# Expert routing of a fused DeltaNet + MoE kernel: started one period later, and its weights computed on GpSimd instead of VectorE

## The chip, the cores and the metric

One NeuronCore of a Trainium2 chip runs the whole kernel. Its engines work side by side, each through its own queue of instructions in program order: TensorE (PE in the profile; PEld is its weight load), VectorE (DVE), ScalarE (ACT), GpSimd (POOL) and SyncE (SP, which issues DMA transfers). The metric is the device time of one execution in microseconds (us).

## The reference

Two blocks follow each other. The first is DeltaNet attention, a recurrence over 768 time steps for 4 batches of 8 heads with head size 48:

```python
for t in range(S):
    kt, vt, bt = (k_n[:, :, t], v[:, :, t], beta[:, :, t, None])
    y[:, :, t] = np.einsum('bhd,bhde->bhe', q[:, :, t], state)
    v_old = np.einsum('bhde,bhd->bhe', state, kt)
    state = state + bt[:, :, :, None] * np.einsum('bhd,bhe->bhde', kt, vt - v_old)
```

Its output, reordered to 3072 tokens of width 384, goes through a two-level mixture of experts. A token picks the best of 4 groups (largest of 4 logits) and, inside the group, the best of 4 experts; its weight is the product of the two softmax values at those places:

```python
g_idx = np.argmax(g_logits, axis=1)      # g_sm = softmax(g_logits), with + 1e-09 in the divisor
e_idx = np.argmax(e_logits, axis=1)      # e_sm = softmax(e_logits), the same
h = np.maximum(xg[mask_e] @ w1[g, e], 0.0)
ye = h @ w2[g, e]
combined = g_w[mask_g][mask_e] * e_w[mask_e]
out[tok_idx] = combined[:, None] * ye
```

## The kernel before

**Stages.** Attention is computed in chunks of 32 time steps, 24 chunks, called u = 0 to 23. One chunk holds 4 batches x 32 steps = 128 tokens. After it the MoE stage goes through the 16 experts one after the other. Between them lies a DRAM array, `x_dram`, that holds the tokens sorted by expert: a token's row is written there by an indirect DMA, and the MoE stage reads an expert's rows from it. The MoE stage can't start before the last of these writes has landed.

**A period of attention.** The loop at L512 emits one *period* per chunk, and one more for the last routing work. Inside a period the work is emitted in a fixed order: the matmuls of chunk u (`advance`, L264: `a_ps`, `o_ps`, then `w_ps`, then `s_ps` and the state `s_bd`, then `o_ps` and the output `x`), the router logits of chunk u - 1 (`logits`, L328: transposes `t_ps`, copy `xt`, matmuls `l_ps`, copy `lg`), the value scaling `vh` of chunk u + 1 (`scale`, L257, on VectorE), and the Gram matrices of chunk u + 9 (`gram`, L162: matmuls `g_ps`, ScalarE copy `gt`, VectorE product `gq`, L184). The tensors `t_ps`, `g_ps` and `r_ps` share one PSUM buffer with the tag "g", so each must be read out before the next is written.

**The elimination.** Every four chunks form a group g, and for each group VectorE inverts the triangular 32x32 systems of the four chunks (`inverse`, L188): a transpose of `gt` into `m` (L194), a clamp (L199), a square root on ScalarE (L201), some short steps, then thirty pairs `t` = product (L233) and `m` += `t` (L237), each waiting for the one before it, a last product (L239) and a transpose into `mt` (L244). ScalarE turns that into `mtb` (L249), which `w_ps` of the group's chunks reads.

**Routing.** The chunks are routed in groups r: r = 0 to 4 of four chunks, r = 5 and 6 of two. `route` (L347) reads the group's logits `lg`, takes maxima `gb`, `eb`, makes one-hot masks `gh`, `eh` (ties broken by the descending constant `desc`), the differences `sx` = (`gx`, `ex`), the joint mask `hot`, and adds `hot` to the running counts `acc` (GpSimd for groups of four, L398). TensorE counts ranks into `r_ps` (L404, L405), ScalarE takes `sx` = exp(`sx`) (L407), VectorE makes the slots `rk`, `slot_i` (L410, L413) and the weight `cw` (L417 to L429: sums `ed`, `gd`, products, a reciprocal). GpSimd copies `cw` into the token rows (L436) and issues the indirect DMA that scatters them (L437); these writes are called *puts* here. GpSimd also writes the row numbers into `x` (L318). There are ten `x` buffers, so a chunk's put must have landed before the chunk ten later writes its `x`.

**What sets the order.** All engines' orders inside attention are written out by hand. `inverse` and `route` are Python generators, kept in a list `behind`; each `yield` is a place where the task may be left. `work(n)` (L464) gives every task n x 180 x share nanoseconds of credit, and pushes tasks by one step while they have credit; a step costs 180, or more where the yield says so. A task that yields a word (`ACT_STEP`, `PE_STEP`, `SOON`, `NEXT`) is held until the loop calls `allow` with it: `NEXT` right after the first part of `advance` in the next period, `PE_STEP` and `ACT_STEP` near a period's end. So an emitted place fixes the order in each engine's queue, and what stands ahead in a queue blocks what is behind it. A routing task starts at the end of the period after its group's last chunk, with share 0.25, or 0.6 and 1 for the last groups:

```python
r = group_of.get(u - 1)
if r is not None and group_of.get(u) != r:
    start(route(r), 0.25 if r < NGR - 2 else 0.6 if r < NGR - 1 else 1)
```

NGR is 6. Where the text names "period 5" it means the pass of the loop with u = 5.

Of the kernel before, what the change touches and what calls it, by code (L numbers as in the profile page):

```python
# [8 lines left out]
F32 = mybir.dt.float32  # L9
I32 = mybir.dt.int32  # L10
AX = mybir.AxisListType
ALU = mybir.AluOpType
# [42 lines left out]
def deltanet_then_moe(  # L55
# [14 lines left out]
    nc = tc.nc  # L70
# [15 lines left out]
    NGR = NCH // RG  # L86
# [33 lines left out]
    with ExitStack() as first:  # L120
        ap_ = first.enter_context(tc.tile_pool(name="attn", bufs=1))
        wk = first.enter_context(tc.tile_pool(name="wk", bufs=2))
        sm = first.enter_context(tc.tile_pool(name="small", bufs=2))
# [201 lines left out]
        group_of = {u: r for r, (u0, n) in enumerate(groups) for u in range(u0, u0 + n)}  # L325
# [21 lines left out]
        def route(r):  # L347


            u0, n = groups[r]  # L350
            us = range(u0, u0 + n)

            def small(name, shape_, dt=F32):
                return sm.tile([128, RG] + shape_, dt, tag=name, name=f"{name}{r}",
                               bufs=3)[:, 0:n]

            lg = lg_.pop(r)[:, 0:n]
            gl, el = lg[:, :, 0:G], lg[:, :, G:NL].rearrange("p n (g e) -> p n g e", g=G)
            gb, eb = small("gb", [1]), small("eb", [G])
            gh, eh = small("gh", [G]), small("eh", [G, EG])  # L360
            gt, et = small("gt", [1]), small("et", [G])
            sx = small("sx", [NL])
            gx, ex = sx[:, :, 0:G], sx[:, :, G:NL].rearrange("p n (g e) -> p n g e", g=G)
            like_g, like_e = [128, n, G], [128, n, G, EG]
            desc_g = cut["desc"].rearrange("p (n e) -> p n e", n=RG)[:, 0:n]
            desc_e = cut["desc"][:, None, 0:G * EG].to_broadcast([128, n, G * EG]).rearrange(
                "p n (g e) -> p n g e", g=G)
            nc.vector.tensor_reduce(gb[:, :, 0], gl, axis=AX.X, op=ALU.max)
            yield
            nc.vector.tensor_reduce(eb, el, axis=AX.X, op=ALU.max)  # L370
            yield
            nc.vector.tensor_tensor(gh, gl, gb.to_broadcast(like_g), op=ALU.is_ge)
            yield
            nc.vector.tensor_tensor(eh, el, eb[:, :, :, None].to_broadcast(like_e), op=ALU.is_ge)
# [9 lines left out]
            nc.vector.tensor_tensor(gh, gh, gt.to_broadcast(like_g), op=ALU.is_equal)  # L384
            yield
            nc.vector.tensor_tensor(eh, eh, et[:, :, :, None].to_broadcast(like_e),
                                    op=ALU.is_equal)
            yield
            nc.vector.tensor_tensor(gx, gl, gb.to_broadcast(like_g), op=ALU.subtract)
            yield  # L390
            nc.vector.tensor_tensor(ex, el, eb[:, :, :, None].to_broadcast(like_e),
                                    op=ALU.subtract)
            yield
            hot = small("hot", [G, EG])
            nc.vector.tensor_tensor(hot, gh[:, :, :, None].to_broadcast(like_e), eh, op=ALU.mult)  # L395
            hotf = hot.rearrange("p n g e -> p n (g e)")
            for g, u in enumerate(us):
                (nc.gpsimd if n == RG else nc.vector).tensor_tensor(  # L398
                    acc[:, u + 1], acc[:, u], hotf[:, g], op=ALU.add)
            if n == RG:  # L400
                yield NEXT
            yield PE_STEP
            r_ps = ps.tile([128, RG, NE], F32, tag="g", name=f"r_ps{r}")[:, 0:n]
            nc.tensor.matmul(r_ps, lhsT=before, rhs=hotf, start=True, stop=False)  # L404
            nc.tensor.matmul(r_ps, lhsT=ones, rhs=acc[:, u0:u0 + n], start=False, stop=True)  # L405
            yield ACT_STEP
            nc.scalar.activation(sx, sx, ACT.Exp)  # L407
            yield NEXT
            rk, slot_i = small("rk", [NE]), small("slot_i", [1], I32)
            nc.vector.tensor_tensor(rk, r_ps, hotf, op=ALU.mult)  # L410
            yield
            with nc.allow_low_precision("sums of whole numbers below 2 ** 24"):
                nc.vector.tensor_reduce(slot_i[:, :, 0], rk, axis=AX.X, op=ALU.add)  # L413
            yield

            gd, ed, cw = small("gd", [1]), small("ed", [G]), small("cw", [1])
            nc.vector.tensor_reduce(ed, ex, axis=AX.X, op=ALU.add)  # L417
            yield
            nc.vector.tensor_reduce(gd[:, :, 0], gx, axis=AX.X, op=ALU.add)
            yield  # L420
            nc.vector.scalar_tensor_tensor(ed, in0=ed, scalar=1e-9, in1=gh, op0=ALU.add,
                                           op1=ALU.mult)
            yield
            nc.vector.tensor_reduce(cw[:, :, 0], ed, axis=AX.X, op=ALU.add)
            yield
            nc.vector.scalar_tensor_tensor(cw, in0=gd, scalar=1e-9, in1=cw, op0=ALU.add,
                                           op1=ALU.mult)
            yield
            nc.vector.reciprocal(cw, cw)  # L429
            yield  # L430
            for g, u in enumerate(us):
                x = xs.pop(u)
                if n == RG:
                    yield
                    yield
# [15 lines left out]
        def start(task, share):  # L451
            behind.append(task)
            rate[task], due[task] = share, 0.0
# [32 lines left out]
        with tc.manual_schedule(engines={mybir.EngineType.PE, mybir.EngineType.DVE,  # L486
# [25 lines left out]
            for u in range(NCH + 1):  # L512
                step = advance(u) if u < NCH else iter([None] * 4)
                turned = logits(u - 1) if u else iter([None] * 2)
                next(step)
                allow(NEXT)
                next(turned)
                if u + 1 < NCH:
                    scale(u + 1)
                work(8)  # L520
                if u % RG == RG - 1 and u // RG + 2 < NGR:
                    start(inverse(u // RG + 2), 1)
                work(8)
# [12 lines left out]
                if r is not None and group_of.get(u) != r:  # L536
                    start(route(r), 0.25 if r < NGR - 2 else 0.6 if r < NGR - 1 else 1)
                allow(SOON)
                work(12)
                if u + NB < NCH:  # L540
                    load_kq(u + NB)
                if u + NV < NCH:
                    load_kv(u + NV)
                if u in (2, 3):
                    weights[u - 2] = load_expert(u - 2)
                if u == 1:
                    for e in range(NE):
                        nc.sync.dma_start(out=slots(e), 
                                          in_=zero[:, None, :].to_broadcast([P, T, XW]))
# [118 lines left out]
    with tc.For_i(0, n_over):  # L668
# [10 lines left out]
                                       op0=ALU.mult, op1=ALU.add)  # L679
# [83 lines left out]
```

## Time and profile before

The median of three runs is 642.9 us (639.74 to 643.19). The profile comes from one further execution that took 636.67 us; its span, from the first to the last instruction, is 634.9 us.

| what | where in the span | us |
|---|---|---|
| set-up and first elimination | 0 to 56 | 56 |
| periods 0 to 3 | 56 to 104 | 48 |
| periods 4 to 7 | 104.77 to 147.45 | 42.7 |
| periods 8 to 11 | 147.45 to 187.81 | 40.4 |
| periods 12 to 15 | 187.81 to 227.21 | 39.4 |
| periods 16 to 19 | 227.21 to 261.16 | 34.0 |
| periods 20 to 23 | 261.16 to 291.80 | 30.6 |
| last routing, puts landing | 291.80 to 304.88 | 13.1 |
| experts | 304.88 to 634.9 | 330.0 |

A period's bounds are the starts of the ScalarE copy `f` (L280). Over the span TensorE is busy 520.8 us, VectorE 248.5, ScalarE 177.9 and GpSimd 75.4. In a timeline a line reads: start, duration, engine, line, operation, output <- inputs, shape, and in brackets the idle time of that engine just before and what ended it. "issue" stands for idle time that no recorded event explains.

### The profile page before, as it was taken

How to read it: one execution, taken by the hardware profiler on the slowest of the kernel's cores; microseconds unless marked ns; L12 is line 12 of the kernel's file. 1: busy time of each engine (PE TensorE's matmuls, PEld its weight loads, DVE VectorE, ACT ScalarE, POOL GpSimd, SP SyncE). 2: the span in 40 equal slices, each digit the busy share in tenths (PEclk: the TensorE clock that was granted, in tenths of full speed). 3: DMA queues.
4: the chain of work that ended last, by engine and by line, in shares of the span. 5: the costliest groups of instructions: out<-in, count | busy, mean ns of one | idle time of the engine just before them, and what ended most of it. 6: DMA issues, size and time to landing. Idle time of an engine off the chain costs nothing. (4 is left out here: it accounts for less than half of the span.)

```text
span 634.9 us, 18041 instructions
## 1 busy us (share of the span) xinstructions
PE 520.8 (82%) x8070; PEld 476.2 (75%) x8070; DVE 248.5 (39%) x744; ACT 177.9 (28%) x336; POOL 75.4 (12%) x136
## 2 busy tenths in 40 slices
PE   2313768888889788883799999999999999999991
PEld 2203546766667666673699999999999999999990
DVE  5688976869959699223011111101111111111000
ACT  2102334474555645541011111111111111111110
POOL 4000000020030301305000111001110001110011
PEclk9999989898979879996699999999999999999996
DMA  8960787353331221302245755656656557556000
GB/s 214 266 208 1 211 261 271 96 145 88 96 107 62 67 75 61 111 4 101 65 158 182 237 180 191 212 153 225 226 159 213 171 189 239 176 198 203 26 15 20
DMA packets 39551, 93.40 MB, mean 147 GB/s; under 512 B 3465, under 2 KB 24002, under 8 KB 39472
## 3 DMA queue, kind: packets, MB, share of 16 engines
q1 hardware_dynamic: 35888, 82.76, 41.7%
q0 software_dynamic: 3584, 9.47, 4.2%
q8 instruction: 64, 1.05, 0.7%
q14 instruction: 15, 0.12, 0.1%
HBM read 77.21 MB, written 15.78 MB: 146 GB/s over the span
## 5 line engine op out<-in xcount | busy, mean ns | idle before, releaser
L597 PE MATMUL h_ps<-xt,w 128*128 128x224 f32 x768 | 155.2, 356 | 0.6 <-DVE xt L588 0.6
L611 PE MATMUL y_ps<-hid,w 128*128 128x224 f32 x768 | 153.3, 353 | 0.0
L597 PEld LDWEIGHTS h_ps<-xt,w 128*128 128x128 f32 x768 | 144.7, 193 | 1.4 <-DVE xt L588 0.9
L611 PEld LDWEIGHTS y_ps<-hid,w 128*128 128x128 f32 x768 | 143.0, 190 | 0.0
L588 DVE COPY xt<-t_ps 128x336 f32<-128x336 f32 x32 | 16.2, 508 | 167.5 <-PE t_ps L586 167.5
L600 ACT ACTIVATE hid<-h_ps 128x448 f32<-128x448 f32 x64 | 34.8, 543 | 140.4 <-PE h_ps L597 140.4
L625 DVE TENSOR_SCALAR yo<-o_ps,xg 112x384 f32<-112x384 f32 x32 | 19.7, 618 | 120.4 <-PE o_ps L622 120.4
L626 POOL DMA_INDIRECT out_dram<-yo,at x32 | 30.1, 941 | 296.9 <-DVE yo L625 237.1
L237 DVE TENSOR_TENSOR m<-m,t 128x30 f32<-128x30 f32 (+9 forms) x180 | 59.6, 331 | 5.1
L233 DVE TENSOR_TENSOR t<-m 128x30 f32<-128x30 f32 (+9 forms) x180 | 59.4, 330 | 4.4
L270 PE MATMUL a_ps<-vh,con 128*128 128x384 f32 x48 | 27.9, 670 | 36.8 <-DVE vh L257 23.9
L613 ACT ACTIVATE yt<-y_ps 128x224 f32<-128x224 f32 x48 | 17.1, 357 | 134.3 <-PE y_ps L611 134.3
L176 PE MATMUL g_ps<-kqt 48*32 48x64 f32 x1536 | 25.3, 260 | 23.1 <-issue 9.5
L308 ACT ACTIVATE s_bd<-s_ps 48x768 f32<-48x768 f32 x46 | 36.9, 803 | 19.6 <-PE s_ps L302 19.0
L176 PEld LDWEIGHTS g_ps<-kqt 48*32 48x32 f32 x1536 | 19.8, 124 | 26.6 <-issue 12.3
L270 PEld LDWEIGHTS a_ps<-vh,con 128*128 128x128 f32 x48 | 8.8, 230 | 39.2 <-DVE vh L257 21.2
L302 PE MATMUL s_ps<-w,kv 32*128 32x96 f32 x736 | 27.8, 286 | 7.5 <-ACT w L295 4.7
L302 PEld LDWEIGHTS s_ps<-w,kv 32*128 32x128 f32 x736 | 23.8, 192 | 10.1 <-ACT w L295 5.7
L292 PEld LDWEIGHTS w_ps<-f,mtb 64*64 64x64 f32 x768 | 25.7, 140 | 7.6 <-issue 5.3
L276 PEld LDWEIGHTS a_ps<-s_bd,kqt 128*32 128x32 f32 x736 | 18.7, 128 | 16.5 <-issue 16.5
L292 PE MATMUL w_ps<-f,mtb 64*64 64x48 f32 x768 | 28.8, 226 | 2.4 <-issue 1.2
L398 POOL TENSOR_TENSOR acc<-acc,hot 128x16 f32<-128x16 f32 x20 | 6.1, 306 | 188.5 <-DVE hot L395 187.4
(92 smaller groups left out, 489.5 us busy)
## 6 DMA issues: line engine op xcount, KB each, us to landing
w<-in_w_dram SPq DMA_DIRECT2D x32, 1536.0 KB, 6.8
kv<-in_kv_dram SPq DMA_DIRECT2D x24, 448.0 KB, 3.8
kqt<-in_kq_dram SPq DMA_DIRECT2D x48, 192.0 KB, 6.6
x_dram<-zero SPq DMA_DIRECT2D x16, 337.8 KB, 8.0
xg<-x_dram SPq DMA_DIRECT2D x16, 337.8 KB, 3.2
con<-in_const_dram SPq DMA_DIRECT2D x1, 755.0 KB, 4.8
out_dram<-yo,at POOLq DMA_INDIRECT x32, 3.5
x_dram<-x,slot_i POOLq DMA_INDIRECT x24, 3.2
```

Of the source, the lines that this page charges most:

```text
L176: nc.tensor.matmul(g_out[quads[b], hh * NP + j], lhsT=kqt[rows, 0, j, quads[b]], rhs=kqt[rows, :, j, quads[b]], start=True, stop=True, ski ...
L233: nc.vector.tensor_tensor(tv, m[:, j + 1:, j:j + 1].to_broadcast([128, n, j]), m[:, j:j + 1, 0:j].to_broadcast([128, n, j]), op=ALU.mult)
L237: nc.vector.tensor_tensor(m[:, j + 1:, 0:j], m[:, j + 1:, 0:j], tv, op=ALU.add)
L270: nc.tensor.matmul(a_ps.rearrange("p h d -> p (h d)"), lhsT=ident, rhs=vh.rearrange("p h d -> p (h d)"), start=True, stop=(u == 0), skip_g ...
L292: nc.tensor.matmul(w_ps[b, h], lhsT=mt[b, uu * H + (h % 2) * NP + h // 2], rhs=f[b, h], start=True, stop=True, skip_group_check=True)
L302: nc.tensor.matmul(s_at[:, b, j], lhsT=k[quads[b], j], rhs=w[quads[b], 2 * j:2 * j + 2], start=(u == 0 and j == 0), stop=True, skip_group_ ...
L308: nc.scalar.activation(s_bd[rows, :, :, hh, :], s_at[rows, :, :, hh * D:(hh + 1) * D], ACT.Copy)
L597: nc.tensor.matmul(h_ps[:, k], lhsT=w1[:, j, (f + k) * 128:(f + k + 1) * 128], rhs=xt[:, j], start=(j == 0), stop=(j == DC - 1), skip_grou ...
L600: nc.scalar.activation(hid[:, f:f + 2], h_ps, ACT.Relu)
L611: nc.tensor.matmul(y_ps, lhsT=w2[:, f, j * 128:(j + 1) * 128], rhs=hid[:, f], start=(f == 0), stop=(f == FC - 1))
L625: nc.vector.tensor_scalar(yo, o_ps, xg[:, i, DM:DM + 1], None, op0=ALU.mult)
L626: nc.gpsimd.indirect_dma_start(out=out[:, :], out_offset=bass.IndirectOffsetOnAxis(ap=at[:, i:i + 1], axis=0), in_=yo[:, :], in_offset=Non ...
```

## The change

Four things are different.

1. The routing of groups 0 to 3 (`slow`) starts one step later: early in the next period, after its `allow(NEXT)`, and no longer at the end of the period before. Groups 4 to 6 still start at a period's end; group 4 has share 0.8 in place of 0.6.
2. For groups 0 to 3 the differences `sx` and the sums and products of the weight are made by GpSimd. A sum over four is two additions there (`total`, with a helper tile `twoe` or `twog`), a fused add-and-multiply is two instructions (`times`). That is 12 more GpSimd instructions a group, and 7 fewer on VectorE.
3. For these groups there is one more `yield NEXT` before the reciprocal, so the reciprocal and the puts come one period later.
4. Group 4 is treated like the two short ones: its count additions `acc` are on VectorE, it does not wait a period before `r_ps`, and there are no empty steps between its puts.

```diff
+            slow = r < NGR - 2
...
+            gb_, gt_ = gb.to_broadcast(like_g), gt.to_broadcast(like_g)
+            eb_, et_ = (t[:, :, :, None].to_broadcast(like_e) for t in (eb, et))
             nc.vector.tensor_reduce(gb[:, :, 0], gl, axis=AX.X, op=ALU.max)
             yield
             nc.vector.tensor_reduce(eb, el, axis=AX.X, op=ALU.max)
             yield
+            side, turn = (nc.gpsimd, ()) if slow else (nc.vector, (0,))
+            if slow:
+                side.tensor_tensor(gx, gl, gb_, op=ALU.subtract)
+                side.tensor_tensor(ex, el, eb_, op=ALU.subtract)
...
-            nc.vector.tensor_tensor(gx, gl, gb.to_broadcast(like_g), op=ALU.subtract)
-            yield
-            nc.vector.tensor_tensor(ex, el, eb[:, :, :, None].to_broadcast(like_e),
-                                    op=ALU.subtract)
-            yield
+            if not slow:
+                side.tensor_tensor(gx, gl, gb_, op=ALU.subtract)
+                yield
+                side.tensor_tensor(ex, el, eb_, op=ALU.subtract)
+                yield
...
-                (nc.gpsimd if n == RG else nc.vector).tensor_tensor(
+                side.tensor_tensor(
                     acc[:, u + 1], acc[:, u], hotf[:, g], op=ALU.add)
-            if n == RG:
+            if slow:
                 yield NEXT
...
-            nc.vector.tensor_reduce(ed, ex, axis=AX.X, op=ALU.add)
-            yield
-            nc.vector.tensor_reduce(gd[:, :, 0], gx, axis=AX.X, op=ALU.add)
-            yield
-            nc.vector.scalar_tensor_tensor(ed, in0=ed, scalar=1e-9, in1=gh, op0=ALU.add,
-                                           op1=ALU.mult)
-            yield
-            nc.vector.tensor_reduce(cw[:, :, 0], ed, axis=AX.X, op=ALU.add)
-            yield
-            nc.vector.scalar_tensor_tensor(cw, in0=gd, scalar=1e-9, in1=cw, op0=ALU.add,
-                                           op1=ALU.mult)
-            yield
+            def total(out, x, name):
+                if not slow:
+                    nc.vector.tensor_reduce(out, x, axis=AX.X, op=ALU.add)
+                    return
+                two = sm.tile(list(out.shape) + [2], F32, tag=name, name=f"{name}{r}")
+                last_of = [slice(None)] * len(out.shape)
+                side.tensor_tensor(two, x[(*last_of, slice(0, 2))], x[(*last_of, slice(2, 4))],
+                                   op=ALU.add)
+                side.tensor_tensor(out, two[(*last_of, 0)], two[(*last_of, 1)], op=ALU.add)
+
+            def times(out, x, y):
+                if not slow:
+                    nc.vector.scalar_tensor_tensor(out, in0=x, scalar=1e-9, in1=y, op0=ALU.add,
+                                                   op1=ALU.mult)
+                    return
+                side.tensor_scalar(x, x, 1e-9, 1.0, op0=ALU.add, op1=ALU.mult)
+                side.tensor_tensor(out, x, y, op=ALU.mult)
+
+            total(ed, ex, "twoe")
+            yield from turn
+            total(gd[:, :, 0], gx, "twog")
+            yield from turn
+            times(ed, ed, gh)
+            yield from turn
+            total(cw[:, :, 0], ed, "twog")
+            yield from turn
+            times(cw, gd, cw)
+            if slow:
+                yield NEXT
             yield
             nc.vector.reciprocal(cw, cw)
             yield
             for g, u in enumerate(us):
                 x = xs.pop(u)
-                if n == RG:
+                if slow:
                     yield
                     yield
...
                 allow(NEXT)
+                r = group_of.get(u - 2)
+                if r is not None and group_of.get(u - 1) != r and r < NGR - 2:
+                    start(route(r), 0.25)
                 next(turned)
...
                 r = group_of.get(u - 1)
-                if r is not None and group_of.get(u) != r:
-                    start(route(r), 0.25 if r < NGR - 2 else 0.6 if r < NGR - 1 else 1)
+                if r is not None and group_of.get(u) != r and r >= NGR - 2:
+                    start(route(r), 0.8 if r == NGR - 2 else 1)
```

In the built program the order on TensorE, ScalarE and SyncE is the same as before for groups 0 to 3; the orders of VectorE and GpSimd differ as told. In VectorE's queue `gb` of these groups moves from before `vh` of the next chunk, two elimination pairs ahead of it, to behind it, and the reciprocal moves from before L194 of period 7 (11, 15) to behind the first `vh` of period 8 (12, 16).

More of the change, by code (lines that the diff above doesn't have):

```diff
@@ L371, in route @@
             yield
-            nc.vector.tensor_tensor(gh, gl, gb.to_broadcast(like_g), op=ALU.is_ge)
+            side, turn = (nc.gpsimd, ()) if slow else (nc.vector, (0,))
+            if slow:
+                side.tensor_tensor(gx, gl, gb_, op=ALU.subtract)
+                side.tensor_tensor(ex, el, eb_, op=ALU.subtract)
+            nc.vector.tensor_tensor(gh, gl, gb_, op=ALU.is_ge)
             yield
-            nc.vector.tensor_tensor(eh, el, eb[:, :, :, None].to_broadcast(like_e), op=ALU.is_ge)
+            nc.vector.tensor_tensor(eh, el, eb_, op=ALU.is_ge)
             yield
@@ L383, in route @@
             yield
-            nc.vector.tensor_tensor(gh, gh, gt.to_broadcast(like_g), op=ALU.is_equal)
+            nc.vector.tensor_tensor(gh, gh, gt_, op=ALU.is_equal)
             yield
-            nc.vector.tensor_tensor(eh, eh, et[:, :, :, None].to_broadcast(like_e),
-                                    op=ALU.is_equal)
+            nc.vector.tensor_tensor(eh, eh, et_, op=ALU.is_equal)
             yield
-            nc.vector.tensor_tensor(gx, gl, gb.to_broadcast(like_g), op=ALU.subtract)
-            yield
-            nc.vector.tensor_tensor(ex, el, eb[:, :, :, None].to_broadcast(like_e),
-                                    op=ALU.subtract)
-            yield
+            if not slow:
[3 more added lines that the diff above has]
+                yield
             hot = small("hot", [G, EG])
```

## The prediction

> **What bounds the kernel now.** I read the busy table by stretch first, then VectorE's waits, then the timeline around each wait. The table of busy time between the starts of `f` of periods 4, 8, 12, 16, 20 and 24 (columns: stretch, length, then busy time of PE, PEld, DVE, ACT and POOL) shows where VectorE can matter:
>
> ```profile
> 104.77:147.45 42.68, 33.73 (x1079) 27.11 (x1072) 34.01 (x108) 22.07 (x38) 6.82 (x16) 0.89 0.48 150
> 147.45:187.81 40.36, 34.38 (x1080) 27.86 (x1076) 32.84 (x105) 22.30 (x39) 6.76 (x16) 0.88 0.37 108
> 187.81:227.21 39.40, 32.88 (x1016) 26.80 (x1012) 32.45 (x104) 21.48 (x38) 6.72 (x16) 0.89 0.22 70
> 261.16:291.80 30.64, 26.30 (x762) 21.58 (x751) 6.81 (x46) 13.91 (x30) 6.49 (x16) 1.00 0.13 44
> ```
>
> Four periods without elimination take 30.6 us, with it 39 to 43. The chain of waits' end is of no use here: it is the 330 us of experts, which the change leaves alone. In each elimination group VectorE runs without a pause from the short steps after the square root to the transpose `mt`, and TensorE ends up waiting for it (`gq`, L184); then ScalarE takes over (`mtb`, table load, square root, state copy) and VectorE waits 3 to 5 us. So a VectorE saving counts only if it lies before `gq` of period 6, 10 or 14, and only if it is not swallowed by an earlier VectorE wait.
>
> The timeline shows which of the moved and removed steps lie there. First the wait that the new start removes, in period 4, and the next VectorE step that must wait for other engines, `gq` of period 5:
>
> ```profile
> 112.78 0.39 DVE L237 TENSOR_TENSOR m<-m,t 128x220 f32<-128x220 f32 x1
> 115.54 0.17 DVE L368 TENSOR_REDUCE gb<-lg 128x4 f32<-128x16 f32 x1 [2.38 <-ACT lg L344]
> 115.62 0.39 DVE L233 TENSOR_TENSOR t<-m 128x228 f32<-128x228 f32 x1
> ...
> 121.31 0.63 ACT L179 ACTIVATE gt<-g_ps 128x256 f32<-128x256 f32 x1 [0.28 <-PE g_ps L176]
> 122.46 0.42 DVE L184 TENSOR_TENSOR gq<-g_ps,con 128x256 f32<-128x256 f32 x1
> ```
>
> The reader is to see that elimination steps stand behind `gb` in VectorE's queue for 2.38 us, though they need nothing of it. Then what an inserted routing step costs among the pairs (period 9):
>
> ```profile
> 153.94 0.39 DVE L233 TENSOR_TENSOR t<-m 128x220 f32<-128x220 f32 x1
> 154.36 0.39 DVE L237 TENSOR_TENSOR m<-m,t 128x220 f32<-128x220 f32 x1
> 154.67 0.16 DVE L368 TENSOR_REDUCE gb<-lg 128x4 f32<-128x16 f32 x1
> 154.78 0.40 DVE L233 TENSOR_TENSOR t<-m 128x228 f32<-128x228 f32 x1
> ```
>
> Start to start is 0.42 us from `t` to `m` without a step between, and 0.42 from `m` to `t` with `gb` between. The step starts in the gap that the dependent pair leaves. Its 0.16 us of busy time costs nothing.
>
> **The change part by part.** The base is the profiled execution, 636.67 us.
>
> *Start of routing (groups 0 to 3).* Only two of the four `gb` waited: 2.38 us (period 4) and 0.22 (period 16). Behind `vh`, `gb` comes after `lg` in all four, so both waits go. What is late next: `gq` of period 5 needs `gt`, which ends at 121.31 + 0.63 = 121.94. `gq` ran at 122.46, so VectorE can gain 122.46 - 121.94 = 0.52, less a hand-over of 0.03 (in the set-up `gt` ended at 33.40 and `gq` began at 33.43): **0.49 us** of the 2.38. In period 6 TensorE waited 0.92 us before `r_ps` for `gq`; this falls to 0.43 and everything behind comes 0.49 earlier. The 0.22 of period 16 counts in full, as `t_ps` of period 19 waited 1.11 for `rk`, which stood behind `mt`: **0.2 us**.
>
> *`sx` on GpSimd.* Two VectorE steps a group, 169 and 219 ns, leave the pairs. By the spacing above they were free: 0 gained. If the cover is not real, 0.39 a group.
>
> *Sums on GpSimd.* Five steps stood in a row before L194: in period 7 `ed` starts at 135.28 and L194 at 136.22, the reciprocal included, so L194 comes 0.94 earlier. Behind L194 and L199 VectorE only waits for the square root (3.07, 3.06 and 5.13 us in periods 7, 11, 15), and that comes after `mtb` in ScalarE's queue, so the 0.94 is swallowed there. The exception is `gt` of period 7, which overwrites what L194 reads: L194 ended at 137.43, and `gt` started 1.34 us after `w`, against 0.93 in period 11, where L194 was done long before (178.77 - 177.84). That is **0.41 us** on ScalarE's chain `w`, `gt`, `mtb`, square root, state copy. Period 15 has no such `gt`, period 19 no elimination: 0 there.
>
> *Reciprocal one period later.* It now stands behind `vh` at the head of the uninterrupted stretch, where a step does cost its spacing, 0.09 (136.13 to 136.22): 3 x 0.1 = **0.3 us lost** (periods 8, 12, 16; in 20 VectorE is idle). It waits for GpSimd, and the elimination pairs and `gq` stand behind it. GpSimd's ten steps start when the exponential ends (134.08) and cost 0.306 each by the row of its count additions (L398: mean 0.306, longest 0.585), 3.1 to 5.9 us: done by 140, while the reciprocal's turn comes at about 146. It becomes a wait only above some 1.2 us a step. The Trainium skill (GPSIMD Engine Reference, § 4.1 Engine selection) speaks against this part: it puts two-input elementwise work at about half VectorE's speed on GpSimd and reductions on VectorE. By that rule the ten steps would be longer, but with six us of room the sum would not change.
>
> *Exponential.* It now waits for GpSimd's `sx`, two steps issued a period earlier: done long before. Same place in ScalarE's queue, same table loads (1.28 us each): 0.
>
> *GpSimd's queue and the puts.* The twelve steps lie ahead of the row-number writes L318 of the next chunks, for which only that chunk's put, two periods on, waits. A group's four puts with their copies (0.20 + 0.99 + gaps, 5.8 us) move from period 7 to period 8, to 147 to 153 us, and land about 3.2 later. `x` of period 10 (171.74) is the first to need such a buffer: 15 us of room. DMA runs at 0.36 share there: 0.
>
> *Beside VectorE's pairs.* New GpSimd work runs while VectorE eliminates. The trace has one such meeting, period 9:
>
> ```profile
> 163.66 0.37 DVE L237 TENSOR_TENSOR m<-m,t 128x210 f32<-128x210 f32 x1
> 163.83 1.47 POOL L398 TENSOR_TENSOR acc<-acc,hot 128x16 f32<-128x16 f32 x4 [19.92 <-DVE hot L395]
> 164.07 0.37 DVE L233 TENSOR_TENSOR t<-m 128x198 f32<-128x198 f32 x1
> 164.47 0.37 DVE L237 TENSOR_TENSOR m<-m,t 128x198 f32<-128x198 f32 x1
> 164.87 0.35 DVE L233 TENSOR_TENSOR t<-m 128x184 f32<-128x184 f32 x1
> ```
>
> VectorE's spacing stays 0.41, 0.40, 0.40 against 0.41 without GpSimd (153.12 to 153.53); GpSimd gives way (0.37 a step against a shortest of 0.219). For the puts only one short meeting exists: L205 to L209 in period 7, beside the last put (142.41), are spaced 0.25 and 0.23, and in period 11 without a put 0.25 and 0.22. I take 0; the upper end is a full stop of VectorE for each of the twelve puts of groups 0 to 2, 12 x 0.99 = 11.9 us. The Trainium skill (SBUF — State Buffer, § Who interferes with whom) is harsher than the first row: a VectorE instruction with two SBUF inputs and a GpSimd instruction that reads SBUF exclude each other, the first holding the port to its end. By that rule the six `sx` steps beside the pairs could cost an estimated 6 x 0.3 = 1.8 us, and the sum would be a loss of 1.0 in place of a gain of 0.8.
>
> *Group 4.* Its steps come a period earlier, with four VectorE additions (0.175 each) in place of GpSimd's. VectorE is busy 6.8 of 30.6 us there and then waits 12.34 for `lg` of the next group: 0, or 0.7 without that cover. `r_ps` moves from the end of period 22 to that of 21, the same 0.8 us of TensorE. The puts leave GpSimd's queue about 8 us earlier, but the stage ends on the last reciprocal: GpSimd idled 1.60 us before the last group's copy (296.44). 0.
>
> Sum: -0.49 - 0.2 - 0.41 + 0.3 = **-0.8 us**, 635.9 on the profiled execution.
>
> **The clock.** In the stretch from 144.30 (`a_ps`) to 148.97 (`w_ps`) TensorE ran at half clock and took 4.67 us; the same steps at full clock in period 9 take 154.50 to 157.28, 2.78. So one half-clock episode costs 1.9 us, and there are seven in the attention stage. A shift of 0.9 us can add or remove one or two.
>
> **To the median.** The four executions shown are 636.67, 639.74, 642.9 and 643.19, mean 640.6; the median of the runs is 642.9. A new median should fall between, 641.8 less 0.8: **641.0 us**. About 0.5% (3.2 us) is what a measurement of this kernel can tell from no change.
>
> **The rivals.**
> *A, likeliest (0.52):* as summed, same within 0.5%. Own range 638 to 643.5, for one half-clock episode and the spread of the runs.
> *B, faster (0.28):* the removed steps are worth more than their spacing says, or shorter stalls spare half-clock episodes. For it: TensorE waited 2.45 us for `gq` in period 14, and every VectorE delay counts there. Against it: the 0.42 spacings. Two episodes fewer give -0.8 - 3.8 = -4.6, 637.2. The upper end: 28 steps by busy time, 4 x (169 + 219 + 203 + 156 + 175 + 170 + 162 ns) = 5.0, plus both `gb` waits in full, 2.6: -7.6, 634.2.
> *C, slower (0.20):* GpSimd's puts, now beside the pairs of periods 8, 12 and 16, hold VectorE up. For it: no row shows a put beside pairs. Against it: the 0.25 and 0.23. It decides from (3.2 + 0.8) / 12 = 0.33 us a put; at half the full stop it is +5.2, 647.0, at the full stop +11.1, 652.9.
> That the change does nothing (`gb` no longer waits, but `gq` does) is inside A, at 641.8.
>
> **How the numbers follow.** The range is 635.5 to 646: it leaves out the end of B (0.06) and most of C (0.14). Faster 0.28, same 0.52, slower 0.20.
>
> **What would show it.** Right: no wait before `gb` of groups 0 to 3; `gq` of period 5 right behind `gt`; TensorE's wait before `r_ps` of period 6 near 0.4; `gt` of period 7 about 0.9 after `w`; 2.5 us of wait before `r_ps` in period 14, as before; reciprocals without a wait. Wrong: a VectorE wait for GpSimd at the reciprocal, pairs spaced wider than 0.42 beside puts or `sx`, or periods 8 to 15 shorter by more than 1 us at equal clock.

## The result, and the profile after

The changed kernel takes as long as the one before: 638.77 us (median of 42 executions, 630.95 to 644.32) against 638.57 us (47 executions, 631.07 to 644.62). The ratio is 1.000, with a 95% interval of 0.9979 to 1.0022. The forecast was "same within 0.5%", 641.0 us in a range of 635.5 to 646.

The execution profiled after took 642.76 us, 6 us more than the one profiled before. The medians show no such difference, so it belongs to the two executions and not to the change. TensorE ran at half clock for 54.6 us of periods 0 to 23 (37.5 us before). Over 44 executions of the changed kernel the time falls by 3.2 us for each 0.01 that the mean granted clock is higher; by that the clocks of the two profiles, 0.932 and 0.945, stand for some 4 of the 6 us.

The table of busy time by stretch, of the changed kernel, between the starts of `f` of periods 4, 8, 12, 16, 20 and 24 (stretch, length, then busy time of PE, PEld, DVE, ACT and POOL, granted clock, DMA share, GB/s):

```profile
104.39:148.50 44.11, 35.25 (x1080) 28.55 (x1072) 33.29 (x100) 22.09 (x39) 4.90 (x19) 0.87 0.42 130
148.50:190.06 41.56, 36.34 (x1080) 29.06 (x1076) 32.17 (x98) 22.25 (x38) 9.99 (x28) 0.83 0.35 105
190.06:229.51 39.45, 33.16 (x1022) 27.15 (x1017) 31.62 (x97) 21.50 (x38) 10.69 (x28) 0.89 0.22 70
265.90:296.40 30.50, 26.42 (x761) 21.81 (x754) 7.47 (x50) 13.99 (x29) 5.23 (x11) 0.98 0.13 44
```

VectorE lost seven or eight instructions and 0.7 to 0.8 us of busy time in each of the first three stretches (34.01 to 33.29 in the first). The stretches did not become shorter: 44.1, 41.6 and 39.5 us against 42.7, 40.4 and 39.4, at a lower clock in the first two.

The timeline of the changed kernel, at the places that the forecast named (only the rows that are read below; "..." stands for a longer stretch between them):

```profile
116.57 0.17 DVE L371 TENSOR_REDUCE gb<-lg 128x4 f32<-128x16 f32 x1 [1.27 <-ACT lg L344]
116.83 0.30 POOL L378 TENSOR_TENSOR sx<-lg,gb 128x16 f32<-128x16 f32 x1 [108.08 <-DVE gb L371]
117.10 0.40 DVE L233 TENSOR_TENSOR t<-m 128x240 f32<-128x240 f32 x1
117.53 0.41 DVE L237 TENSOR_TENSOR m<-m,t 128x240 f32<-128x240 f32 x1
117.97 0.41 DVE L233 TENSOR_TENSOR t<-m 128x240 f32<-128x240 f32 x1
...
123.34 0.61 ACT L179 ACTIVATE gt<-g_ps 128x256 f32<-128x256 f32 x1 [0.29 <-PE g_ps L176]
123.99 0.42 DVE L184 TENSOR_TENSOR gq<-g_ps,con 128x256 f32<-128x256 f32 x1 [2.95 <-ACT gt L179]
...
134.22 0.43 PE L411 MATMUL r_ps<-hot,con 128*128 128x64 f32 x2 [0.45 <-DVE gq L184]
...
138.63 0.49 ACT L295 ACTIVATE w<-w_ps 128x384 f32<-128x384 f32 x1 [0.58 <-PE w_ps L292]
139.45 0.62 ACT L179 ACTIVATE gt<-g_ps 128x256 f32<-128x256 f32 x1 [0.34 <-PE g_ps L176]
...
148.15 0.55 DVE L257 TENSOR_TENSOR vh<-kv,normt 128x384 f32<-128x384 f32 x1
148.62 0.17 DVE L456 RECIPROCAL cw<-cw 128x4 f32<-128x4 f32 x1
148.71 0.19 DVE L233 TENSOR_TENSOR t<-m 128x58 f32<-128x58 f32 x1
...
151.66 1.06 PE L176 MATMUL g_ps<-kqt 48*32 48x64 f32 x64
151.70 0.97 POOL L464 DMA_INDIRECT x_dram<-x,slot_i  x1 [0.28 <-POOL x L463]
152.76 0.61 ACT L179 ACTIVATE gt<-g_ps 128x256 f32<-128x256 f32 x1 [0.49 <-PE g_ps L176]
...
214.52 0.43 PE L411 MATMUL r_ps<-hot,con 128*128 128x64 f32 x2 [2.36 <-DVE gq L184]
```

From the top: the wait for the logits fell to 1.27 us, and the time reappears at `gq`, which now waits 2.95 us for `gt` and runs 0.04 us behind its end. VectorE's pairs are spaced 0.43 and 0.44 us while GpSimd makes `sx`. That is no widening: a step of this size (128x240) has the same spacing before, where GpSimd is idle beside it, as 118.59 to 119.04 in the kernel before:

```profile
118.59 0.41 DVE L233 TENSOR_TENSOR t<-m 128x240 f32<-128x240 f32 x1
119.04 0.41 DVE L237 TENSOR_TENSOR m<-m,t 128x240 f32<-128x240 f32 x1
```

The reciprocal takes 0.09 us between `vh` and the next `t`, without a wait. While GpSimd issues the second put (151.70), the 64 Gram matmuls pass in 1.06 us and ScalarE follows them 0.04 us later; remember these two lines for the experiments.

One figure sums VectorE's side up. I took, for each of the four groups that run beside attention, the time from the start of `m` times `r0` (L223) to the start of the product with `cs` (L239), less the waits in brackets between them. It is 25.76, 25.73, 25.75 and 25.36 us before, and 25.88, 25.86, 25.81 and 25.39 after. With two instructions fewer in it, a reciprocal more in three of the four, and GpSimd's work beside it, it came out 0.03 to 0.13 longer: the instructions that left it gave nothing that shows.

### The profile page after: what moved, and what is told of

Its sections match the earlier page's. It is cut to its first block, busy times and chain, and to the rows that moved or that the text cites. A ratio compares the mean times of both kernels' runs of the same rounds, so it can differ in the third digit from the quotient of the medians.

```text
span 640.5 us, 18039 instructions
## 1 busy us (share of the span) xinstructions
PE 528.3 (82%) x8070; PEld 482.6 (75%) x8070; DVE 246.1 (38%) x720; ACT 178.4 (28%) x336; POOL 88.6 (14%) x180
## 5 line engine op out<-in xcount | busy, mean ns | idle before, releaser
L302 PE MATMUL s_ps<-w,kv 32*128 32x96 f32 x736 | 30.1, 303 | 7.8 <-ACT w L295 4.7
L302 PEld LDWEIGHTS s_ps<-w,kv 32*128 32x128 f32 x736 | 25.8, 206 | 10.4 <-ACT w L295 5.7
L276 PEld LDWEIGHTS a_ps<-s_bd,kqt 128*32 128x32 f32 x736 | 20.0, 134 | 17.4 <-issue 17.4
L313 PE MATMUL o_ps<-w,gq 32*32 32x48 f32 x1536 | 25.2, 215 | 2.8 <-issue 2.7
```

The source lines that it names most:

```text
L302: nc.tensor.matmul(s_at[:, b, j], lhsT=k[quads[b], j], rhs=w[quads[b], 2 * j:2 * j + 2], start=(u == 0 and j == 0), stop=True, skip_group_ ...
L313: nc.tensor.matmul(o_ps[b, h], lhsT=gq[b, (h % 2) * NP + h // 2], rhs=w[b, h], start=(u == 0 and h == 0), stop=True, skip_group_check=True)
```

## The experiments

Theory A is the forecast's: what the change takes off VectorE was free. Three sets of four kernels ran, each set on one chip with its own runs of the kernel before (medians 653.59, 652.32 and 654.35 us). These three chips, called first, second and third here, are some 2% slower than the runs of the result; the last set shows where most of that lies. All ratios are to the kernel before on the same chip, with 95% intervals.

| kernel | median us | ratio | interval |
|---|---|---|---|
| later start alone | 650.73 | 0.9966 | 0.9930 to 1.0002 |
| GpSimd part alone | 658.89 | 1.0079 | 1.0047 to 1.0111 |
| one filler a gap | 661.39 | 1.0105 | 1.0041 to 1.0169 |
| two fillers a gap | 669.01 | 1.0250 | 1.0185 to 1.0315 |
| changed kernel again | 656.37 | 1.0053 | 1.0011 to 1.0094 |
| late delay | 657.59 | 1.0073 | 1.0035 to 1.0110 |
| early delay | 654.74 | 1.0055 | 1.0022 to 1.0088 |
| changed, root on VectorE | 650.75 | 0.9955 | 0.9915 to 0.9995 |
| kernel before again | 654.50 | 1.0016 | 0.9977 to 1.0055 |
| changed, without 16 puts | 641.04 | 0.9804 | 0.9738 to 0.9869 |
| before, without 16 puts | 639.85 | 0.9789 | 0.9723 to 0.9855 |
| before, root on VectorE | 648.88 | 0.9925 | 0.9890 to 0.9959 |

### The two halves of the change

The later start alone, against the kernel before:

```diff
                 allow(NEXT)
+                r = group_of.get(u - 2)
+                if r is not None and group_of.get(u - 1) != r and r < NGR - 2:
+                    start(route(r), 0.25)
...
-                if r is not None and group_of.get(u) != r:
-                    start(route(r), 0.25 if r < NGR - 2 else 0.6 if r < NGR - 1 else 1)
+                if r is not None and group_of.get(u) != r and r >= NGR - 2:
+                    start(route(r), 0.6 if r < NGR - 1 else 1)
```

The GpSimd part alone (items 2 to 4 of the change, with the start of before), against the changed kernel:

```diff
-                r = group_of.get(u - 2)
-                if r is not None and group_of.get(u - 1) != r and r < NGR - 2:
-                    start(route(r), 0.25)
...
-                if r is not None and group_of.get(u) != r and r >= NGR - 2:
-                    start(route(r), 0.8 if r == NGR - 2 else 1)
+                if r is not None and group_of.get(u) != r:
+                    start(route(r), 0.25 if r < NGR - 2 else 0.8 if r == NGR - 2 else 1)
```

> The kernel before with the later start of routing alone; sx, sums and puts as before. Theory A (what the change takes off VectorE was free, because an independent step fits into the gap of a dependent pair and the wait for the logits is replaced by the wait of gq for the Gram matmuls): time within 0.5% of before; the waits of gb mostly gone, gq of period 5 directly behind gt; the steps after the square root spaced as before, t to m about 0.42 with or without a routing step between. Rival B (VectorE's busy time and waits count, and only the clock hides it): 2.6 us faster than before, both gb waits in full.

> The changed kernel with the start of routing of before: sx, sums, reciprocal a period later and group 4 as in the change. Theory A: within 0.5% of before (sum -0.1 us: 0.41 gained at gt of period 7, 0.3 lost at the reciprocals); gb of period 4 waits 2.4 us again; no wait of VectorE for GpSimd at the reciprocal. Rival B: 5.0 us faster, the busy time of the 28 removed steps. Rival C (GpSimd's new work holds VectorE up): slower by 1.8 us or more, with pairs spaced over 0.45 us while GpSimd runs.

The later start gave 0.34%, just not distinguishable from nothing and inside 0.5%, as A expected. The GpSimd part alone cost 0.79%, which A did not expect: 5.3 us by medians. Rival B's gain of 5.0 us is refuted. Rival C, that GpSimd holds VectorE up, is not what happened either: VectorE's figure from L223 to L239 is 26.04, 26.11, 26.08 and 25.48 us, 0.15 to 0.4 above the kernel before on the third chip (25.86, 25.73, 25.74 and 25.33), some 1 us in all; and its pairs of 128x220 keep 0.42 us beside GpSimd's work. Most of the loss lies elsewhere. The waits inside the same four stretches, which that figure leaves out, are 3.94, 5.17, 4.06 and 1.72 us, against 3.89, 0, 0 and 0 in the kernel before on the third chip, and all of them are for `gt` or for the logits, so for TensorE and ScalarE. The puts that moved now fall into the second to fourth of these stretches; what they do there is shown below. How much of the 5.3 us comes from them, and how much from the later reciprocal or from group 4, no run separates.

### What a small VectorE step costs among the pairs

```diff
+                nc.vector.tensor_reduce(
+                    scr[:, (4 * j + 0) % 256], cut["desc"][:, 0:16].rearrange("p (a b) -> p a b", b=4),
+                    axis=AX.X, op=ALU.max)
                 yield n * j
                 nc.vector.tensor_tensor(m[:, j + 1:, 0:j], m[:, j + 1:, 0:j], tv, op=ALU.add)
+                nc.vector.tensor_reduce(
+                    scr[:, (4 * j + 2) % 256], cut["desc"][:, 0:16].rearrange("p (a b) -> p a b", b=4),
+                    axis=AX.X, op=ALU.max)
                 yield n * j
```

With two fillers each of these stands twice, on scratch columns of its own.

> The changed kernel with a small independent VectorE step (a maximum over 128x16, its result unused) after every t and every m of the elimination: 60 more a group, 360 in all, 240 of them in the four groups that run beside attention. Theory A: pairs of 128x220 stay at 0.42 us start to start; only where the gap already holds a step does the second cost some 0.1, about 15 places a group: 0 to 6 us slower. Rival B: each costs its 0.16 us: 38 us slower for the four groups, and up to 19 more in the set-up.

> As the kernel with one filler, but two behind every t and every m: 120 more a group. Theory A: the first is free and the second costs its own spacing of 0.09 to 0.11 us, 60 a group: the pairs of 128x220 spaced 0.5 to 0.53, four groups 24 us slower, up to 12 more in the set-up. Rival B: 77 us slower in the four groups. If the gap is larger than one small step, it costs nearly nothing.

VectorE's timeline of the kernel with one filler:

```profile
208.36 0.39 DVE L235 TENSOR_TENSOR t<-m 128x220 f32<-128x220 f32 x1
208.66 0.16 DVE L238 TENSOR_REDUCE scr<-con 128x4 f32<-128x16 f32 x1
208.78 0.39 DVE L242 TENSOR_TENSOR m<-m,t 128x220 f32<-128x220 f32 x1
209.09 0.16 DVE L243 TENSOR_REDUCE scr<-con 128x4 f32<-128x16 f32 x1
209.20 0.40 DVE L235 TENSOR_TENSOR t<-m 128x228 f32<-128x228 f32 x1
```

With a filler in every gap `t` to `m` is still 0.42 us. From the product with `r0` to the product with `cs`, waits left out, the four groups take 26.81, 27.02, 26.97 and 26.31 us; the changed kernel on the second chip takes 25.85, 26.05, 25.99 and 25.39. So 60 steps that are busy for some 9.5 us cost 0.9 to 1.0 us: 0.016 us a step. The second filler costs 0.04 a step (29.33 against 26.81 in the first group, 60 more steps), where A had expected 0.09 to 0.11. Rival B, that busy time counts, is refuted by a factor of ten for one filler. In time one filler costs 0.5% over the changed kernel, and two cost 2.0%, 13 us where A had expected 24 or more; both are ratios from two chips.

### Ten steps behind the square root, and ten ahead of it

The late delay, and then the early one:

```diff
             nc.vector.reciprocal(r1, r0)
+            for _ in range(10):
+                nc.vector.tensor_tensor(scr, scr, scr, op=ALU.mult)
             yield
```

```diff
+            for _ in range(10):
+                nc.vector.tensor_tensor(scr, scr, scr, op=ALU.mult)
             nc.vector.tensor_tensor(r0, diag, cut["tiny"].to_broadcast([128, C]), op=ALU.max)
```

> The changed kernel itself, on the same chip as the three delay and root kernels below. Theory A: 0.5% or less from before. If the two halves of the change add up (0.34% gained by the later start alone, 0.79% lost by the GpSimd half alone), it is 0.45% slower.

> The changed kernel with ten dependent VectorE steps on a scratch tile (128x32, about 0.23 us each, 2.3 us a group) right behind the first reciprocal after the square root. Theory A (from there to the transpose mt VectorE is what TensorE ends up waiting for, so a delay counts in full): 2.3 us for each of the four groups beside attention and for the first of the set-up, 9 to 14 us slower than the changed kernel. Rival D (TensorE is the bound and VectorE has slack): under 4 us.

> The same ten steps, but between the transpose into m and the clamp ahead of the square root, where the sums of the weight stood before the change. Theory A (there VectorE only waits for ScalarE's square root, 3 to 6 us): swallowed beside attention, 2.3 us from the first group of the set-up, 0 to 5 us slower than the changed kernel. Rival B (busy time counts wherever it lies): as with the late delay.

VectorE's waits between 98 and 306 us (in total, times, longest), of the changed kernel, then of the late delay, then of the early one:

```profile
DVE gq L184 <- ACT gt L179: 16.9, 7, 3.9
DVE r L203 <- ACT r L201: 10.6, 3, 4.5
```

```profile
DVE r L205 <- ACT r L203: 10.6, 3, 4.5
DVE gq L186 <- ACT gt L181: 9.4, 5, 2.9
```

```profile
DVE gq L186 <- ACT gt L181: 11.7, 7, 3.2
DVE r L207 <- ACT r L205: 8.4, 3, 3.1
```

The changed kernel itself was 0.53% slower than before on this chip: A's bound is just missed, and the two halves of the change (0.45% together) add up within their intervals. The ten steps took some 2.2 us and put off what followed by 2.0. Ahead of the square root they cost nothing (1.0055 against 1.0053), as A said, but mostly not in the wait that A named. In periods 7 and 11 they went into the wait of `gq` for `gt`, which stands between the clamp and the square root (1.81 and 3.94 us in the changed kernel, 0 and 0.90 here), and only in period 15 into the wait for the square root (4.48 to 2.45). Behind the square root A expected 9 to 14 us and it was 1.2 by medians (1.0073 against 1.0053): rival D is right here. The waits show where the delay went: `gq` waits 7.5 us less. Between L223 and L239 the waits were 3.88, 3.58 and 4.02 us in the first three groups, and 0, 2.46 and 3.01 with the delay; so these three groups took all of their delay, 6.0 us, out of waits for TensorE and ScalarE. The wait in the first group is there on the chip of the result as well (2.38 us before, 4.22 after). Those of the second and third group are not, neither before nor after: on this chip VectorE's stretch has slack there that it had not in the profile of before.

### Where that slack comes from: the puts

```diff
+                if slow:
+                    yield
+                    continue
                 put = nc.gpsimd.indirect_dma_start(
```

This is the edit of the changed kernel; in the kernel before the condition is `r < NGR - 2`. Most token rows are then never written, so these two kernels are for measuring alone.

The timeline of the changed kernel, run again on the second chip, at the same place as above (period 8, matmuls of `g_ps` and the ScalarE copy `gt`):

```profile
149.05 0.41 PE L176 MATMUL g_ps<-kqt 48*32 48x64 f32 x18
149.74 0.59 PE L176 MATMUL g_ps<-kqt 48*32 48x64 f32 x34 [0.28 <-issue]
150.12 0.97 POOL L464 DMA_INDIRECT x_dram<-x,slot_i  x1 [0.28 <-POOL x L463]
150.72 0.33 PE L176 MATMUL g_ps<-kqt 48*32 48x64 f32 x4 [0.39 <-issue]
151.46 0.32 PE L176 MATMUL g_ps<-kqt 48*32 48x64 f32 x4 [0.41 <-issue]
152.20 0.32 PE L176 MATMUL g_ps<-kqt 48*32 48x64 f32 x4 [0.42 <-issue]
...
154.58 0.61 ACT L179 ACTIVATE gt<-g_ps 128x256 f32<-128x256 f32 x1 [4.22 <-remote]
155.22 0.42 DVE L184 TENSOR_TENSOR gq<-g_ps,con 128x256 f32<-128x256 f32 x1 [3.17 <-ACT gt L179]
```

The 64 matmuls take 3.5 us, not 1.06, and near their end come four at a time, each four followed by a pause that no recorded event explains. ScalarE stands 4.22 us before `gt`, again without a recorded event, and `gq` on VectorE waits for that. All of it falls into the time of the four puts (148.45 to 154.02) and half a us behind. So the question was put whether the puts are the cause:

> The kernel before itself, for its trace beside those of the other runs of this study and as a measure of the comparison. Theory E (while GpSimd issues a group's four puts, the instruction supply of TensorE and ScalarE stalls; in the changed kernel the puts lie in periods 8, 12 and 16 beside the Gram matmuls, here in 7, 11 and 15, where ScalarE runs few long steps and TensorE waits for it): ratio 1.00 within 0.4%; no ScalarE wait without a releaser over 2 us beside the puts of periods 7, 11 and 15, and fewer TensorE stalls there than the 1.0 to 2.0 us a group of the changed kernel. Rival F (the stalls don't depend on where the puts lie): the same stalls as there.

> The changed kernel without the sixteen puts of groups 0 to 3 (left out: most token rows are never written for the experts; the copies of the weight stay). Theory E: the ScalarE waits of 3 to 5 us without a releaser and TensorE's stalls of 0.3 to 0.4 us each in periods 8, 12, 16 and 20 are gone, 4 to 10 us faster than the changed kernel, that is 1 to 7 us faster than before. Rival F: within 2 us of the changed kernel.

> The kernel before without the same sixteen puts (left out as there). Theory E: 0 to 4 us faster than before, and within 0.4% of the changed kernel without puts: the difference of the two kernels lies in where the puts run. Rival F: as far below the changed kernel without puts as before is below the changed kernel, 0.5%.

Without the puts, the same place in the changed kernel; `gq` follows there without a wait:

```profile
150.82 0.86 PE L176 MATMUL g_ps<-kqt 48*32 48x64 f32 x64
...
151.71 0.62 ACT L179 ACTIVATE gt<-g_ps 128x256 f32<-128x256 f32 x1 [0.29 <-PE g_ps L176]
```

And the kernel before with its puts, on the third chip, period 11:

```profile
180.77 0.32 PE L176 MATMUL g_ps<-kqt 48*32 48x64 f32 x4 [0.43 <-ACT xt L338]
181.51 0.47 PE L176 MATMUL g_ps<-kqt 48*32 48x64 f32 x22 [0.42 <-issue]
...
183.17 0.49 ACT L295 ACTIVATE w<-w_ps 128x384 f32<-128x384 f32 x1 [2.62 <-remote]
183.19 0.76 PE L176 MATMUL g_ps<-kqt 48*32 48x64 f32 x33 [0.46 <-issue]
```

Adding up the idle time between 98 and 306 us that stands as "issue" on TensorE, and as "issue" or "remote" on ScalarE, gives:

| kernel, chip | TensorE us | ScalarE us |
|---|---|---|
| before, chip of the result | 7.7 | 1.1 |
| changed, chip of the result | 7.2 | 0.8 |
| before, third chip | 14.4 | 7.6 |
| changed, second chip | 12.6 | 9.2 |
| before without puts, third chip | 6.8 | 3.5 |
| changed without puts, third chip | 6.7 | 0 |

The 3.5 of the fifth row is one wait at 285 us, beside a put of group 4, which that kernel still has.

The puts are the cause of these stalls: taking them away removes them, and with them the slack of the delays' second and third group, where the changed kernel without puts has no wait at all between L223 and L239 (3.58 and 4.02 us with them). Leaving out takes the issue on GpSimd, the transfer and the writes away together; the runs do not say which of these does it. It leaves the changed kernel 13.3 and the kernel before 14.5 us below the kernel before with them. About 1.5 us of that lies behind attention, where fewer rows are written: from the first `hid` to the end took 320.7 us in both profiles, against 322.2 and 322.4 with puts. The rest, some 12 to 13 us for 16 puts, is 0.7 to 0.8 us a put. Not all of it need be the stalls themselves: the mean granted clock is higher without the puts too (0.936 against 0.925 in the kernel before), which by the 3.2 us for each 0.01 above, an estimate carried over from the chip of the result, goes with some 3.5 us. It also closes most of the gap between the chips: without puts the kernel before takes 639.85 us on a chip of the experiments, and 638.57 with them in the runs of the result, where the two profiles show no such stall. Why the puts stall TensorE and ScalarE on some chips and not on others the runs do not tell.

Theory E was right that the puts stall the two engines and that both kernels come out equal without them (0.9804 and 0.9789). It was wrong that the old place of the puts is much better: the kernel before stalls beside them too (2.62 us on ScalarE in period 11, where E had forecast none over 2), so that rival F is right in this, and in the kernel before they cost as much. Both sizes were far too small: 13.3 us below before where E expected 1 to 7, and 14.5 where it expected 0 to 4. Whether their place explains the 0.5% that separates the two kernels on these chips stays open: the difference without puts is 0.15%, but known only to 0.9%.

### The square root on VectorE

```diff
-            nc.scalar.activation(r0, r0, ACT.Sqrt)
+            r0_i = r0.bitcast(I32)
+            nc.vector.tensor_scalar(r0_i, r0_i, 1, None, op0=ALU.arith_shift_right)
+            nc.vector.tensor_scalar(r0_i, r0_i, 0x1FBD1E00, None, op0=ALU.add)
+            nc.vector.reciprocal(r1, r0)
+            nc.vector.tensor_tensor(r1, r1, diag, op=ALU.mult)
+            nc.vector.tensor_tensor(r0, r0, r1, op=ALU.add)
+            nc.vector.tensor_scalar(r0, r0, 0.5, None, op0=ALU.mult)
```

Each new step is followed by a `yield`; the two that held the task at ScalarE's place (`ACT_STEP`, `SOON`) go. The one ScalarE step ahead of attention that loads the table of the square root loads that of the exponential.

> The changed kernel with the square root made by VectorE: a first estimate from the number's bits (a shift and an addition) and one more Newton round, in place of ScalarE's square root; ScalarE then keeps the table of the exponential and loads none beside attention. Takes away the square root wait of VectorE (3.1, 3.1 and 6.0 us in periods 7, 11 and 15) and, ahead of the state copy on ScalarE, 1.5 us of table load and square root in four periods; adds six steps, some 1.3 us a group. Theory A (VectorE's elimination and that ScalarE chain bound these periods): 5 to 12 us faster than the changed kernel. Rival D (TensorE bounds): under 3 us.

> The kernel before, all its routing included, with the square root made by VectorE as in the changed kernel with that root. A version that may beat both: theory A gives 0.5 to 1.3% faster than before, 3 to 8 us, as the same edit gave 0.98% on the changed kernel. Rival D (TensorE bounds, the gain was the puts' luck): within 0.4% of before.

On the changed kernel the edit gave 5.6 us (656.37 to 650.75), which is A's lower end, and on the kernel before 5.5 (654.35 to 648.88): 0.75%, with an interval from 0.4 to 1.1%, as A said. The kernel before with the root on VectorE is the fastest, against before, of the versions that compute everything. Of VectorE's square root waits none is left (10.6 us in the changed kernel, 15.0 in the one before), and a part comes back at `gq`. Here are the waits between 98 and 306 us of the kernel before, run again, and then of the kernel before with that root:

```profile
DVE r L203 <- ACT r L201: 15.0, 3, 8.9
DVE gq L184 <- ACT gt L179: 10.2, 3, 6.9
```

```profile
DVE gq L184 <- ACT gt L179: 14.6, 7, 5.1
```

That is some 4 us more at `gq`. The gain also fits ScalarE, whose busy time up to the first `hid` falls from 125.9 to 116.3 us, 9.0 of it table loads. The runs do not separate VectorE's share from ScalarE's.

## Why the prediction was right, point by point

*What the removed steps are worth.* Right, and the best supported step: an independent step in the gap of a dependent pair costs 0.016 us, not 0.16. That the sums' 0.94 us ahead of the square root were swallowed is supported by the early delay, whose 2.0 us a group were, on another chip. But "VectorE only waits for the square root" there left out `gq`, which stands between in periods 7 and 11 and took the delay in both.

*Start of routing.* Half right. "So both waits go" failed for group 0: TensorE was at half clock there, VectorE came to `gb` before the logits, and 1.27 us of wait stayed. What is late next was right: `gq` ran at the end of `gt`, TensorE's wait before `r_ps` of period 6 was 0.45 (0.43 forecast), and that of period 14 stayed, 2.36 for 2.45. The 0.2 us of period 16 is not seen: `gb` no longer waits there, but TensorE's wait for `rk` before `t_ps` of period 19, which was to fall from 1.11 us, is 2.33 in the profile after, at a lower clock in that stretch (0.87 against 0.96).

*`gt` of period 7.* It started 0.82 us after `w`, forecast 0.9. *Reciprocal.* It took 0.09 us, without a wait on the chip of the result; on the second chip that of period 20 waited 2.8 us for GpSimd, with no elimination behind it. *GpSimd's ten steps* took 2.85 us (136.20 to 139.05), under the forecast's 3.1 to 5.9.

*Beside VectorE's pairs.* Right that neither `sx` nor the puts hold VectorE up: on the chip of the result its stretch grew by at most 0.13 us a group, the reciprocal's 0.09 included, and on the chips of the experiments by up to 0.4. The rule of exclusion of the Trainium skill (SBUF — State Buffer, § Who interferes with whom) did not show: the forecast's estimate by it was 1.8 us for six `sx` steps, and in the built program eight stand beside pairs. But the list of whom the puts can hold up was too short. It had VectorE in it, and not TensorE and ScalarE; rival C's size, 0.33 us a put to decide, was reached on other chips by an effect on these two. It did not decide there because the kernel before pays it too. On the second chip the same forecast would have met a ratio of 1.0053, just outside its "same within 0.5%", for a cause that stays open; that the profiles of the result show no such stall is luck.

*"A VectorE saving counts only if it lies before `gq` of period 6, 10 or 14"* was not tried on the chip of the result: the 0.49 us that came earlier at `gq` is too little to show in the time. On the second chip it does not hold in the other direction: there even a loss of 2.0 us a group is absorbed, in three of the four groups.

*The time.* The sum of -0.8 us lies within the interval (1.4 us either way) and can't be told from 0. The 641.0 was 2.2 too high because its base leant on three executions with a median of 642.9; 47 have 638.57. So the verdict "same" is sound, but that the median came out within 2.2 us says little for the sum. The spread of 631 to 644 within one kernel, most of which goes with the granted clock, is far larger than what was forecast.

## What to carry to other kernels

Before moving short steps off an engine, look at the spacing of what they stand between: in this chain of dependent instructions a gap took one of them at a tenth of its busy time (0.016 of 0.16 us) and a second at a quarter, and the busy total told nothing. A wait that is removed reappears at the next instruction of the queue that needs the same late engine, so look for that one first. A transfer issued by GpSimd can cost engines that have nothing to do with it (0.7 to 0.8 us a put here, on some chips); price it by leaving it out.

## What was not expected of the hardware

On the three chips of the experiments, while GpSimd issues indirect writes, TensorE in places runs only four matmuls, then pauses 0.4 us, again and again. ScalarE stops once for 1.9 to 5.4 us beside 24 of the 40 groups of four puts of routing groups 0 to 3 in the ten profiles there that have them. Leaving 16 puts out saves 12 to 13 us of attention. The Trainium skill (Runtime: NRT & Kernel Launch, § Instruction fetch mechanics) says that every engine streams its instructions through a DMA queue of its own in blocks, and that crossing a block is mostly hidden. The pauses would fit instructions that arrive late because of the puts, but no run here shows the fetch itself, and in the two profiles of the result they do not occur.

Much of the spread of one kernel goes with the granted clock: over 44 executions of the changed kernel, mean clocks of 0.924 to 0.955 go with 644 to 631 us, and the straight line through them leaves a standard deviation of 1.8 us of 3.3. In the two profiles of the result half clock comes in lengths of 3.41, 6.83, 10.24 and 20.48 us, so 3.4 us and its multiples, but for the last of each, which ends with the program (14.2 and 14.4 us).
